# Linear attention into a gated feed-forward layer on one core: MoE chunks that end at token tiles, and the remainders of both quads as one unit

## The chip, the cores and the metric

The kernel runs on one core of a Trainium2 chip. The time is that of one execution on the device, in microseconds; lower is better. A core has TensorE (PE: matmuls; its loading of stationary operands is shown apart as PEld), VectorE (DVE), ScalarE (ACT), GpSimd (POOL), SyncE (SP: issues the DMAs here), an on-chip memory SBUF of 128 partitions, and 8 accumulator banks (PSUM) that TensorE writes and VectorE and ScalarE read.

## What is computed

```python
# 8 batches, 8 heads, 576 tokens, head dimension 64, 128 features; all float32
def phi(x):
    proj = np.einsum('bhsd,df->bhsf', x, w_phi)
    proj = proj - np.max(np.abs(proj), axis=-1, keepdims=True)
    return np.concatenate([np.exp(proj), np.exp(-proj)], axis=-1)
q_p, k_p = phi(q), phi(k)
kv = np.einsum('bhsf,bhsd->bhfd', k_p, v)
z = np.sum(k_p, axis=2)
num = np.einsum('bhsf,bhfd->bhsd', q_p, kv)
den = np.einsum('bhsf,bhf->bhs', q_p, z)[..., None] + 1e-06
x = (num / den).transpose(0, 2, 1, 3).reshape(B, S, 512)     # 8 x 576 tokens, 512 wide
h = np.maximum(x @ w_in, 0.0)                                 # 512 -> 1024
conv_out = sum(conv_w[k] * shift(h, k - 1) for k in range(3)) # over tokens, zeros at a batch's ends
gate = 1.0 / (1.0 + np.exp(-conv_out))
out = h * gate @ w_out                                        # 1024 -> 512
```

(The sum over shifts is the reference's loop over the three taps, written short.)

## The kernel before

**Attention.** The 8 heads of a batch form two *quads* (qd 0 and 1) of four heads; a quad is two pairs of two heads each, laid side by side in the partitions (64 + 64). A head's 576 tokens are four tiles of 128 and a remainder of 64. A *unit* is one batch, one quad, and one of three token groups: h = 1 and h = 2 hold two full tiles of both pairs, h = 0 the remainders of both pairs. `k_unit` loads keys and values, projects (`project`: pk), takes the largest absolute value (mk, L433, VectorE), subtracts it (sk, L440, VectorE), makes both exponentials (ke, L464, ScalarE; batch 0 by a bias instead, L468), and accumulates features times values (kv, L477 and L484, TensorE). After h = 2 the sums go to SBUF (kvf, L491). `q_unit` projects likewise (pq, mq, sq), transposes on TensorE (tp, L509), makes the exponentials (qe, L513), multiplies by kvf (nm, L524), and divides on VectorE (dn, rc, x).

TensorE works in three tilings: the whole array (128 x 128: transpositions, MoE, and the remainder's projection L413, one matmul of 256 columns for a quad), halves (128 x 64: kv, nm) and quarters (64 x 64: the projections of full tiles, L422, four at a time). A float32 matmul shows in the profile as two records.

**MoE.** The tokens of two batches are cut into three *chunks* of 384; there are 12. `x_part` transposes a chunk's token tiles on TensorE (xt, L564; a tile of which only a column or a few are needed goes as a matmul by part of the identity, L566) and splits the result into a rounded part and the rest (xh on ScalarE, xl on VectorE), 386 columns, since the convolution looks one token to each side. `h_part` has 8 groups f of 12 matmuls (hp, L594: 4 slices p of the width, three products each of the split weights and x), the relu (h, L598, ScalarE), the middle tap on GpSimd (c, L599), the two others on VectorE (L606), one sigmoid for the chunk (L611, ScalarE; it needs a change of the function table, 12 of them), the gate (L614, VectorE), and the split into gh (ScalarE) and gl (VectorE). `o_part` has 4 x 24 matmuls (op, L644), an eviction (os, L649) and the store. The weights come as 64-bit numbers and are rounded in the first part of the run on VectorE, ScalarE and GpSimd (w_t, win_lo, wout_lo).

**Order.** Every operation is put on a list with its engine, an expected cost, its reads and writes, and a rank. `Plan.order` then plays the list: at each step it takes the engine that can start earliest, and there, among what could start at that moment, the lowest rank; on TensorE `mode` stays in a tiling while something is ready for it. What comes out is the order on each engine, fixed in the program. Buffers have a number of slots, and an operation whose tile finds none free is put later: hidden tiles h have NHH slots, kv uses two PSUM banks, hp and op share two (M), and the other four (G) serve the rest.

Of the kernel before, what the change touches and what calls it, by code (L numbers as in the profile page):

```python
# [245 lines left out]
def kernel(  # L246
# [143 lines left out]
    QUAD = 470  # L390

    def project(src, b, qd, h, kind, r):
# [3 lines left out]
        if h == 0:  # L396
            raw = [piece([P, P], F32, f"r{nm}", "raw", RAW)]
            dma(lambda: raw[0](), lambda: src[b, qd, :, 512 : 512 + P], 64, r - 3.0, writes=w_(raw[0]))
            ps = [psum([P, 2 * F], f"p{nm}", G)]
            n = 2  # L400
        else:
            raw = [piece([P, 2 * P], F32, f"r{nm}_{pr}", "raw", RAW) for pr in range(2)]
            for pr in range(2):
# [4 lines left out]
            n = 4
        m = [piece([P, 2, n], F32, f"m{nm}_{i}", "m", 6) for i in range(len(ps))]
        pr_ = [None if biased else piece([P, n, F], F32, f"s{nm}_{i}", kind + "s", KS if kind == "k" else QS)  # L410
               for i in range(len(ps))]
        if h == 0:
            mm(432, lambda: nc.tensor.matmul(out=ps[0](), lhsT=raw[0](), rhs=wbd_f(), start=True, stop=True),  # L413
               w_(raw[0], wbd_f), w_(ps[0]), r, takes=(m[0],) if biased else (m[0], pr_[0]))
# [336 lines left out]
```

## Time and profile before

| | |
|---|---|
| time, median of 3 runs | 734.47 us (734.21 to 734.63) |
| the profiled execution: its time, its span | 734.25 us, 732.5 us |
| TensorE busy | 715.0 us, 98% of the span |
| VectorE busy | 491.1 us, 67% |
| ScalarE busy | 392.3 us, 54% |
| GpSimd busy | 104.7 us, 14% |
| granted TensorE clock | full, all the time |
| moved by DMA | 49.02 MB |

The span reaches from the first to the last instruction; the time adds 1.75 us around it. A group's row gives line, engine, operation, what is written from what, shapes and count, then busy time in us and mean duration in ns of one, then the idle time of the engine just before them and what ended it. Matmuls overlap in the array, so a mean duration is longer than the step from one start to the next.

### The profile page before, as it was taken

The numbers are of one execution on the slowest core, as the hardware profiler recorded it, in microseconds if no ns is written. First come the engines' busy times: TensorE is split into PE (matmuls) and PEld (weight loads), VectorE is DVE, ScalarE is ACT, GpSimd is POOL, SyncE is SP. The second block draws the span as 40 slices with busy tenths as digits, with TensorE's granted clock in tenths as the row PEclk, the third lists the DMA queues.
The fourth block names the chain that finished last, engine by engine and source line by source line (L and its number), as shares of the span: only waits on it lengthen the run. The fifth ranks groups of instructions, "written<-read, shape, count | busy, mean of one in ns | idle before, by whom it ended". The sixth has DMA issues, their size and how long they took to land.

```text
span 732.5 us, 22234 instructions
## 1 busy us (share of the span) xinstructions
PE 715.0 (98%) x9548; PEld 674.1 (92%) x9548; DVE 491.1 (67%) x1066; ACT 392.3 (54%) x740; POOL 104.7 (14%) x135
## 2 busy tenths in 40 slices
PE   8878999999999999999999999999999999999997
PEld 6767988899999999999999999999999999999997
DVE  3699899999685546657656687568574655576450
ACT  6976676874646426536435554554563544436251
POOL 1233334242001020010010002010001101020100
PEclk9999999999999999999999999999999999999999
DMA  8454444221230201103221231023121010000011
GB/s 239 129 173 135 140 138 129 64 72 37 82 100 18 60 12 60 49 11 93 71 59 33 79 88 42 33 79 85 46 66 34 19 34 17 27 2 34 12 33 44
DMA packets 46610, 49.02 MB, mean 67 GB/s; under 512 B 5296, under 2 KB 44464, under 8 KB 46512
## 3 DMA queue, kind: packets, MB, share of 16 engines
q1 hardware_dynamic: 46512, 47.59, 22.2%
q8 instruction: 76, 1.25, 0.7%
q14 instruction: 22, 0.18, 0.1%
HBM read 38.13 MB, written 9.44 MB: 65 GB/s over the span
## 4 chain that ended last, share of the span: by engine, by line
PE 89%; ACT 5%; DVE 4%; DMA 0%; issue 0%; POOL 0%; SPq 0%; ACTq 0%
PE op L644 28%; PE hp L594 27%; PE nm L524 9%; PE kv L484 6%; PE tp L509 4%; PE pq L422 4%; PE pk L422 3%; PE xt L564 3%; ACT ke L468 3%; PE kv L477 2%; PE pk L413 1%; PE pq L413 1%; DVE mk L433 1%; DVE mq L433 0%; DMA rk<-in_kT_dram 0%; DVE w_t L329 0%
## 5 line engine op out<-in xcount | busy, mean ns | idle before, releaser
L606 DVE SCALAR_TENSOR_TENSOR c<-h,cw,c 128x384 f32<-128x384 f32 (+3 forms) x256 | 128.9, 530 | 82.8 <-POOL c L599 81.0
L594 PE MATMUL hp<-xh,win_hi 128*128 128x386 f32 x384 | 136.1, 355 | 0.0
L644 PE MATMUL op<-gh,wout_hi 128*128 128x384 f32 x384 | 133.4, 347 | 0.0
L599 POOL TENSOR_SCALAR c<-h,cw 128x384 f32<-128x384 f32 x96 | 61.8, 646 | 498.0 <-ACT h L598 449.4
L594 PE MATMUL hp<-xl,win_hi 128*128 128x386 f32 x384 | 130.1, 339 | 1.1 <-DVE xl L572 1.1
L644 PE MATMUL op<-gl,wout_hi 128*128 128x384 f32 x384 | 130.2, 339 | 0.0
L594 PE MATMUL hp<-xh,win_lo 128*128 128x386 f32 x384 | 129.9, 338 | 0.0
L644 PE MATMUL op<-gh,wout_lo 128*128 128x384 f32 x384 | 129.6, 337 | 0.0
L598 ACT ACTIVATE h<-hp 128x386 f32<-128x386 f32 x96 | 47.2, 494 | 127.2 <-PE hp L594 127.1
L464 ACT ACTIVATE ke<-sk 128x512 f32<-128x512 f32 (+1 forms) x140 | 74.8, 594 | 51.2 <-DVE sk L440 28.8
L513 ACT ACTIVATE qe<-tp 128x512 f32<-128x512 f32 (+1 forms) x160 | 79.6, 570 | 35.0 <-PE tp L509 34.7
L524 PEld LDWEIGHTS nm<-kvf,qe 128*64 128x64 f32 x2304 | 71.9, 138 | 12.3 <-issue 9.4
L524 PE MATMUL nm<-kvf,qe 128*64 128x65 f32 x2304 | 79.2, 224 | 3.2 <-DVE sk L440 1.8
L594 PEld LDWEIGHTS hp<-xh,win_hi 128*128 128x128 f32 x384 | 72.3, 188 | 2.1 <-issue 1.2
L594 PEld LDWEIGHTS hp<-xl,win_hi 128*128 128x128 f32 x384 | 72.3, 188 | 1.5 <-DVE xl L572 1.5
L644 PEld LDWEIGHTS op<-gh,wout_hi 128*128 128x128 f32 x384 | 72.2, 188 | 1.5 <-issue 1.0
L594 PEld LDWEIGHTS hp<-xh,win_lo 128*128 128x128 f32 x384 | 72.5, 189 | 0.3
L644 PEld LDWEIGHTS op<-gl,wout_hi 128*128 128x128 f32 x384 | 72.1, 188 | 0.2 <-DVE gl L626 0.2
L644 PEld LDWEIGHTS op<-gh,wout_lo 128*128 128x128 f32 x384 | 72.2, 188 | 0.1
L484 PE MATMUL kv<-v,ke 128*64 128x65 f32 x2048 | 71.3, 223 | 0.3 <-ACT ke L468 0.2
L484 PEld LDWEIGHTS kv<-v,ke 128*64 128x64 f32 x2048 | 65.4, 138 | 4.4 <-ACT ke L468 1.7
L433 DVE TENSOR_REDUCE mq<-pq 128x4 f32<-128x512 f32 (+1 forms) x80 | 48.6, 630 | 30.1 <-PE pq L422 20.8
(62 smaller groups left out, 960.9 us busy)
## 6 DMA issues: line engine op xcount, KB each, us to landing
v<-in_vt_dram SPq DMA_DIRECT2D x80, 130.0 KB, 2.3
rk<-in_kT_dram SPq DMA_DIRECT2D x64, 128.0 KB, 2.5
rq<-in_qT_dram SPq DMA_DIRECT2D x64, 128.0 KB, 2.3
out_dram<-os SPq DMA_DIRECT2D x32, 192.0 KB, 1.9
w_r<-in_w_in_dram SPq DMA_DIRECT2D x8, 512.0 KB, 3.9
w_r<-in_w_out_dram SPq DMA_DIRECT2D x8, 512.0 KB, 3.9
out_dram<-os SPq DMA_DIRECT2D x32, 96.0 KB, 1.7
rk<-in_kT_dram SPq DMA_DIRECT2D x16, 64.0 KB, 2.5
```

What stands on the lines that cost most here:

```text
L422: nc.tensor.matmul(out=ps[i]()[a : a + 64, (2 * pr + t) * F : (2 * pr + t + 1) * F], lhsT=raw[pr]()[rows, t * P + a : t * P + a + 64], rhs ...
L433: lambda i=i, view=view: nc.vector.tensor_reduce(out=m[i]()[:, 0], in_=view(), axis=AX, op=ALU.max, apply_absolute_value=True), w_(p), [(m ...
L464: act(*((630, 522) if n == 4 else (416, 307)), lambda s=s, e=e, j=j: nc.scalar.activation(out=e[s](), in_=pr[j](), func=AF.Exp, scale=1.0 ...
L484: nc.tensor.matmul(out=kp[j]()[a : a + 64, s, t // 2 * VW : (t // 2 + 1) * VW], lhsT=e[s]()[:, t, a : a + 64], rhs=vs[t // 2]()[:, c : c + ...
L509: nc.tensor.transpose(out=tp()[:, t, :], in_=pr[j]()[:, t, :], identity=idn())
L513: act(*((597, 478) if n == 4 else (384, 264)), lambda s=s, tp=tp, qe=qe: nc.scalar.activation(out=qe()[:, s], in_=tp(), func=AF.Exp, scale ...
L524: nc.tensor.matmul(out=ps_()[a : a + 64, t, :], lhsT=qe()[:, s, t, a : a + 64], rhs=kv[b, qd][t if h == 0 else j]()[:, s, p0 : p0 + VW], s ...
L594: nc.tensor.matmul(out=ps(), lhsT=w, rhs=x, start=(p == 0 and k == 0), stop=(p == 3 and k == 2))
L598: act(494, 373, lambda ps=ps, hs=hs: nc.scalar.activation(out=hs(), in_=ps(), func=AF.Relu), w_(ps), w_(hs), rf)
L599: pool(590, 557, lambda f=f, hs=hs: nc.gpsimd.tensor_scalar(out=c4()[:, f, :], in0=hs()[:, o : o + TC], scalar1=cwv()[:, f, 1:2], scalar2= ...
L606: lambda f=f, hs=hs, j=j, lo=lo, hi=hi: nc.vector.scalar_tensor_tensor(out=c4()[:, f, lo:hi], in0=hs()[:, o + j - 1 + lo : o + j - 1 + hi] ...
L644: nc.tensor.matmul(out=ps(), lhsT=w, rhs=x, start=(i == 0), stop=(i == 23))
```

## The change

Chunks now follow the token stream of all batches (4608 tokens) and end where a token tile ends: 11 chunks, of 384, 448 or 320 tokens. A chunk's hidden layer is computed for its own columns alone. The convolution's output lags two tokens behind the chunk's end (but not at a batch's end), and the three hidden columns that the next chunk needs from this one are copied by GpSimd into the front of its hidden tile. The remainders of both quads of a batch form one unit (k or q), projected in quarters like the full tiles. xh and xl are tiles of their own for each p. Numbers of slots change (hidden tiles 10 to 9, x 8 to 6, raw 6 to 5, v 4 to 2 and two for the remainder, qe 2 to 3), and so do the planner's costs and ranks (of which a few lines stand here).

```diff
-TC = 384
-HW = TC + 2
-HSTART = (0, 383, 766)
-NCH = 12
+EDGE = [64 * n for n in (0, 6, 13, 20, 27, 33, 40, 47, 54, 60, 67, 72)]
+NCH = len(EDGE) - 1
+HW = 448
+TC = HW + 2
-QORDER = [(0, 1), (1, 1), (0, 2), (1, 2), (0, 0), (1, 0)]
+QORDER = [(0, 1), (1, 1), (0, 2), (1, 2), (0, 0)]
+KORDER = [(0, 0), (0, 1), (0, 2), (1, 1), (1, 2)]
-LEAD = 36.0
+LEAD = 42.0
-NHH = 10
+NHH = 9
 def project(src, b, qd, h, kind, r):
-        if h == 0:
-            raw = [piece([P, P], F32, f"r{nm}", "raw", RAW)]
-            dma(lambda: raw[0](), lambda: src[b, qd, :, 512 : 512 + P], 64, r - 3.0, writes=w_(raw[0]))
-            ps = [psum([P, 2 * F], f"p{nm}", G)]
...
-            mm(432, lambda: nc.tensor.matmul(out=ps[0](), lhsT=raw[0](), rhs=wbd_f(), start=True, stop=True),
-               w_(raw[0], wbd_f), w_(ps[0]), r, takes=(m[0],) if biased else (m[0], pr_[0]))
+        n, w = (1, P) if h == 0 else (2, 2 * P)
+        for u in range(2):
+            q, c0 = (u, 512) if h == 0 else (qd, u * 640 + (h - 1) * 256)
+            dma(lambda u=u: raw[u](), lambda q=q, c0=c0: src[b, q, :, c0 : c0 + w], w // 2, r - 3.0, writes=w_(raw[u]))
...
+        def emit(u):
+            for t in range(n):
+                for a in (0, 64):
+                    for i in range(2):
+                        rows = slice(i * D, i * D + D)
+                        nc.tensor.matmul(out=ps[i]()[a : a + 64, (n * u + t) * F : (n * u + t + 1) * F],
+                                         lhsT=raw[u]()[rows, t * P + a : t * P + a + 64],
+                                         rhs=wbd_f()[rows, i * F : i * F + F], start=True, stop=True)
+def around(n):
+        w0, w1 = EDGE[n], EDGE[n + 1]
+        a, z = w0 - 2 * (w0 % S > 0), w1 - 2 * (w1 % S > 0)
...
 def x_part(n, r):
+        tiles = [(b, t, b * S + t * P - w0) for b in range(B) for t in range(5) if w0 <= b * S + t * P < w1]
...
-                    if first + col - i >= 0 and first + col - i + P <= 512:
-                        nc.tensor.transpose(out=xt()[:, first + col - i : first + col - i + P], in_=x, identity=idn())
-                    else:
-                        nc.tensor.matmul(out=xt()[:, first + col : first + col + w], lhsT=x, rhs=idn()[:, i : i + w],
-                                         start=True, stop=True)
+                    nc.tensor.transpose(out=xt()[:, at : at + P], in_=q()[:, qd if t == 4 else 2 * pr + t % 2],
+                                        identity=idn())
 def h_part(n, r):
-                        nc.tensor.matmul(out=ps(), lhsT=w, rhs=x, start=(p == 0 and k == 0), stop=(p == 3 and k == 2))
+                        nc.tensor.matmul(out=ps()[:, :W], lhsT=w, rhs=x, start=(p == 0 and k == 0),
+                                         stop=(p == 3 and k == 2))
+            if t0 < w0:
+                old = hold[f]
+                pool(130, 100, lambda hs=hs, old=old: nc.gpsimd.tensor_copy(
+                    out=hs()[:, :3], in_=old[0]()[:, w0 - old[1] : w0 - old[1] + 3]), [(old[0], "h")], [(hs, "carry")], rf)
```

In k's remainder unit the products with the values (L477 before, L466 now) are issued for one quad after the other, 8 matmuls each as before. The order on the engines changes throughout; three places follow. In the names the first number after the letters is the batch (or the chunk, for xt, hp, h, c and op), then quad and group.

TensorE, the key remainders of batch 5 before: one for each quad, each one matmul of the whole array, the second 157 rows behind the first.

```order
L422 MATMUL pq4_0_1_1_5243<-wbd_f_66,rq4_0_1_1_4646 64x128
L413 MATMUL pk5_0_0_5262<-wbd_f_66,rk5_0_0_4688 128x256
L644 MATMUL op3_3_5230<-gh3_0_4702,wout_hi2_2021 128x384
...
L509 MATMUL tp4_0_2_1_5747<-idn_111,sq4_0_2_1_5711 128x128 x4
L413 MATMUL pk5_1_0_5756<-wbd_f_66,rk5_1_0_5446 128x256
L594 MATMUL hp5_0_5759<-xh5_5602,win_hi0_236 128x386
```

The same remainders now:

```order
L597 MATMUL hp3_2_4760<-xl3_0_4450,win_hi0_374 128x448
L409 MATMUL pk5_0_0_0_4767<-wbd_f_66,rk5_0_0_0_4653 64x128
L409 MATMUL pk5_0_0_1_4769<-wbd_f_66,rk5_0_0_0_4653 64x128
L409 MATMUL pk5_0_0_0_4767<-wbd_f_66,rk5_0_0_0_4653 64x128
L409 MATMUL pk5_0_0_1_4769<-wbd_f_66,rk5_0_0_0_4653 64x128
L409 MATMUL pk5_0_0_0_4767<-wbd_f_66,rk5_0_0_1_4687 64x128
L409 MATMUL pk5_0_0_1_4769<-wbd_f_66,rk5_0_0_1_4687 64x128
L409 MATMUL pk5_0_0_0_4767<-wbd_f_66,rk5_0_0_1_4687 64x128
L409 MATMUL pk5_0_0_1_4769<-wbd_f_66,rk5_0_0_1_4687 64x128
L480 MATMUL kv4_1_0_4234<-v4_1_2_0_4626,ke4_1_2_0_1_4723 64x65 x4
```

Two whole-array matmuls became eight in quarters, between whole-array and half-array work.

TensorE, the second chunk's transpositions (chunk 1, its first slice p) and its last hidden group with the first output matmul behind it, before:

```order
L564 MATMUL xt1_0_2133<-idn_111,x0_0_0_1413 128x128
L566 MATMUL xt1_0_2133<-idn_111,x0_0_2_1070 128x1
L564 MATMUL xt1_0_2133<-idn_111,x0_0_2_1070 128x128
L564 MATMUL xt1_0_2133<-idn_111,x1_0_1_1736 128x128 x2
...
L594 MATMUL hp1_7_3108<-xl1_2187,win_hi3_787 128x386
L644 MATMUL op0_0_3133<-gh0_0_2729,wout_hi0_1561 128x384
```

and now:

```order
L568 MATMUL xt1_0_2573<-idn_91,x0_0_0_1352 128x128
L568 MATMUL xt1_0_2573<-idn_91,x0_0_2_1008 128x128
L568 MATMUL xt1_0_2573<-idn_91,x1_0_1_1632 128x128 x2
...
L597 MATMUL hp1_7_3583<-xl1_3_2810,win_hi3_913 128x448
L654 MATMUL op0_0_3605<-gh0_0_3148,wout_hi0_1630 128x382
```

The single column is gone, and the matmuls are wider. Ahead of that first output matmul stand, now, pq3_1_1 and pk4_0_1; before, pk3_1_1 came only behind it.

GpSimd, the end of the first chunk's middle tap and the start of the second's, before:

```order
L599 TENSOR_SCALAR c0_1557<-h0_7_2470,cw_240 128x384
L343 TENSOR_TENSOR w13_t_2351<-w13_t_2351 128x512
L386 TENSOR_TENSOR wout_lo5_2525<-w13_t_2351,wout_hi5_2512 128x512
L343 TENSOR_TENSOR w14_t_2523<-w14_t_2523 128x512
L386 TENSOR_TENSOR wout_lo6_2789<-w14_t_2523,wout_hi6_2766 128x512
L343 TENSOR_TENSOR w15_t_2533<-w15_t_2533 128x512
L386 TENSOR_TENSOR wout_lo7_2947<-w15_t_2533,wout_hi7_2924 128x512
L599 TENSOR_SCALAR c1_3014<-h1_0_2569,cw_240 128x384
```

and now:

```order
L609 TENSOR_SCALAR c0_1628<-h0_7_2591,cw_235 128x382
L343 TENSOR_TENSOR w12_t_2485<-w12_t_2485 128x512
L604 COPY h1_1_2749<-h0_1_1608 128x3
...
L604 COPY h1_7_2798<-h0_7_2591 128x3
L386 TENSOR_TENSOR wout_lo4_2801<-w12_t_2485,wout_hi4_2795 128x512
L604 COPY h2_0_2883<-h1_0_2467 128x3
L343 TENSOR_TENSOR w13_t_2733<-w13_t_2733 128x512
L386 TENSOR_TENSOR wout_lo5_3003<-w13_t_2733,wout_hi5_2979 128x512
```

The copies of the carried columns stand in the queue ahead of the rounding of the last output weights.

More of the change, by code (lines that the diff above doesn't have):

```diff
@@ L409, in project @@
[L409 to L413, printed above, removed]
-               w_(raw[0], wbd_f), w_(ps[0]), r, takes=(m[0],) if biased else (m[0], pr_[0]))
-        else:
-            def emit(pr):
-                for t in range(2):
-                    for a in (0, 64):
-                        for i in range(2):
-                            rows = slice(i * D, i * D + D)
-                            nc.tensor.matmul(out=ps[i]()[a : a + 64, (2 * pr + t) * F : (2 * pr + t + 1) * F],
-                                             lhsT=raw[pr]()[rows, t * P + a : t * P + a + 64],
-                                             rhs=wbd_f()[rows, i * F : i * F + F], start=True, stop=True)
-            for pr in range(2):
-                mm(QUAD, lambda pr=pr: emit(pr), w_(raw[pr], wbd_f), [(ps[0], pr), (ps[1], pr)], r + 0.01 * pr,
-                   takes=[x for x in (*m, *pr_) if x is not None], tiled=2)
@@ L429, in project @@
+        for u in range(2):
+            mm(225 * n, lambda u=u: emit(u), w_(raw[u], wbd_f), [(ps[0], u), (ps[1], u)], r + 0.01 * u,
+               takes=[x for x in (*m, *pr) if x is not None], tiled=2)
         for i, p in enumerate(ps):
[L430 removed]
+            ri = r + n * i
             view = lambda p=p: p().rearrange("p (t f) -> p t f", f=F)
[L432 removed]
+            vec(*((681, 597) if n == 2 else (417, 331)),
                 lambda i=i, view=view: nc.vector.tensor_reduce(out=m[i]()[:, 0], in_=view(), axis=AX, op=ALU.max,
@@ new lines, in around, with cols @@
+    def around(n):
+        w0, w1 = EDGE[n], EDGE[n + 1]
+        a, z = w0 - 2 * (w0 % S > 0), w1 - 2 * (w1 % S > 0)
+        spans = []
+        for k in (0, 1):
+            cut = sorted({a, z, *(t for b in range(B + 1) for t in (b * S - k, b * S - k + 1) if a <= t <= z)})
+            spans.append([(lo, hi) for lo, hi in zip(cut, cut[1:]) if not (hi == lo + 1 and (lo + k) % S == 0)])
+        return w0, w1, a, z, spans
+    def cols(fixed, each, n, more):
+        return fixed + each * n + more, fixed + each * n
@@ L569, in x_part @@
-            mm(115 * len(tiles), emit, w_(idn, *dict.fromkeys(xs[q] for q in src)), w_(xt), r, takes=(xh[n], xl[n]))
-            act(494, 373, lambda p=p, first=first, xt=xt: nc.scalar.activation(
-                out=xh[n]()[:, p], in_=xt()[:, first : first + HW], func=AF.Copy), w_(xt), [(xh[n], p)], r)
-            vec(550, 466, lambda p=p, first=first, xt=xt: nc.vector.tensor_tensor(
-                out=xl[n]()[:, p], in0=xt()[:, first : first + HW], in1=xh[n]()[:, p].bitcast(F32),
-                op=ALU.subtract), [(xt, None), (xh[n], p)], [(xl[n], p)], r)
@@ L576, with emit @@
-    gt = {}
+            src = [xs[b, qd, 0 if t == 4 else 1 + t // 2] for b, t, _ in tiles]
+            def emit(qd=qd, pr=pr, src=src, first=first, xt=xt):
+                for (b, t, c), q in zip(tiles, src):
+                    at = first + c - (pr * 64 if t == 4 else 0)
+                    nc.tensor.transpose(out=xt()[:, at : at + P], in_=q()[:, qd if t == 4 else 2 * pr + t % 2],
+                                        identity=idn())
+            mm(109 * len(tiles), emit, w_(idn, *dict.fromkeys(src)), w_(xt), r, takes=(xh[n, p], xl[n, p]))
```

239 lines of the change are left out of this document (118 added, 121 removed).

## The prediction

> **What bounds the kernel now.** I read the page first: share of each engine, the slices, the chain that ended last. TensorE is busy for 715.0 of 732.5 us and carries 89% of the chain; its slices stand at 9 from the fifth to the last but one, at full clock. VectorE is the only other engine near its limit, and only in slices 3 to 10 (each is 18.3 us).
>
> ```profile
> PE 715.0 (98%) x9548; PEld 674.1 (92%) x9548; DVE 491.1 (67%) x1066; ACT 392.3 (54%) x740; POOL 104.7 (14%) x135
> PE   8878999999999999999999999999999999999997
> DVE  3699899999685546657656687568574655576450
> PEclk9999999999999999999999999999999999999999
> PE 89%; ACT 5%; DVE 4%; DMA 0%; issue 0%; POOL 0%; SPq 0%; ACTq 0%
> ```
>
> Then the busy times by stage. The columns are the stretch, its length, and busy time with instruction count of PE, PEld, DVE, ACT, POOL.
>
> ```profile
> 0.00:70.00 70.00, 58.66 (x1219) 49.01 (x1219) 50.45 (x107) 54.07 (x150) 18.69 (x21) 1.00 0.60 174
> 70.00:180.00 110.00, 107.62 (x1834) 98.51 (x1834) 104.59 (x231) 73.72 (x141) 37.75 (x34) 1.00 0.34 98
> 180.00:728.00 548.00, 548.00 (x6496) 526.17 (x6495) 336.10 (x730) 264.02 (x449) 48.22 (x80) 1.00 0.16 47
> 728.00:732.50 4.50, 0.73 (x5) 0.40 (x3) 0.00 (x0) 0.49 (x1) 0.00 (x0) 1.00 0.12 44
> ```
>
> From 180 to 728 us TensorE never idles: a microsecond of its work removed there is a microsecond of time. From 70 to 180 it idles for 2.4 us, beside a VectorE that is busy for 104.6 of 110. Before 70 us it idles for 11.3 us and waits for others, so work removed there buys nothing unless the waits go too. The last 4 us are the final eviction and its store. Of all that TensorE waits for, the list of waits has a result of VectorE at the top (time in all, times, longest):
>
> ```profile
> PE tp L509 <- DVE sq L440: 1.9, 2, 1.4
> ```
>
> **The change part by part.** Because matmuls overlap, I price them by the step from one start to the next, not by their durations. First the remainder units. Groups by line, and the same two groups in the first 70 us alone, count the records (two records are one float32 matmul here: 16 units, 32 records of each kind):
>
> ```profile
> L413 PE MATMUL pk<-wbd_f,rk 128*128 128x256 f32 x32 | 10.7, 418 | 2.5 <-DMA rk<-in_kT_dram 1.4 <-DVE mk L433 1.0
> L413 PE MATMUL pq<-wbd_f,rq 128*128 128x256 f32 x32 | 9.6, 386 | 0.5 <-PE hp L594 0.5
> ...
> L413 PE MATMUL pk<-wbd_f,rk 128*128 128x256 f32 x8 | 3.3, 494 | 2.5 <-DMA rk<-in_kT_dram 1.4 <-DVE mk L433 1.0
> L413 PE MATMUL pq<-wbd_f,rq 128*128 128x256 f32 x4 | 1.3, 398 | 0.0
> ```
>
> Timeline rows (start, length, line, what, count) give the steps:
>
> ```profile
> 250.73 0.59 PE L413 MATMUL pk<-wbd_f,rk 128*128 128x256 f32 x2
> 251.16 1.47 PE L564 MATMUL xt<-idn,x 128*128 128x128 f32 x12
> 252.39 0.42 PE L644 MATMUL op<-gh,wout_hi 128*128 128x384 f32 x1
> 252.65 0.34 PE L644 MATMUL op<-gh,wout_lo 128*128 128x384 f32 x1
> ...
> 439.17 0.34 PE L594 MATMUL hp<-xh,win_hi 128*128 128x386 f32 x1
> 439.35 0.33 PE L594 MATMUL hp<-xh,win_lo 128*128 128x386 f32 x1
> 439.52 0.34 PE L594 MATMUL hp<-xl,win_hi 128*128 128x386 f32 x1
> 439.79 1.10 PE L422 MATMUL pq<-wbd_f,rq 64*64 64x128 f32 x32
> 440.71 1.05 PE L422 MATMUL pk<-wbd_f,rk 64*64 64x128 f32 x32
> 441.70 1.11 PE L477 MATMUL kv<-v,ke 128*64 128x130 f32 x16
> 442.74 0.45 PE L594 MATMUL hp<-xh,win_hi 128*128 128x386 f32 x1
> 443.03 0.34 PE L594 MATMUL hp<-xh,win_lo 128*128 128x386 f32 x1
> ```
>
> A whole-array remainder projection holds TensorE from 250.73 to 251.16, 0.43 us; two of them, one for each quad, 0.86. The merged unit has 8 quarter matmuls, 16 records. A run of 32 such records that is followed by more of them takes 439.79 to 440.71, 0.92 us, so 16 take 0.46. The saving is 0.40 us for each of 16 merged units: **-6.4 us**. Their reductions, subtractions and exponentials keep their number and width, and so do the remainder matmuls with the values and the transpositions of q; the stores and loads are a few more on a queue whose engines are busy for at most a third after 70 us, and I cost them at nothing.
>
> Second, the transpositions of x. Chunks of 386 columns cut token tiles: a chunk needs 4, 5 and 4 tiles in turn (13 for two batches), and in the second kind one is a matmul of a single column. Where chunks end at tile ends there are 40 tiles, 160 transpositions instead of 192 and no single columns.
>
> ```profile
> L564 PE MATMUL xt<-idn,x 128*128 128x128 f32 x192 | 27.9, 276 | 1.0 <-ACT qe L513 0.9
> L566 PE MATMUL xt<-idn,x 128*128 128x1 f32 x32 | 4.5, 209 | 0.0
> ...
> 300.49 0.63 PE L564 MATMUL xt<-idn,x 128*128 128x128 f32 x4
> 300.96 0.28 PE L566 MATMUL xt<-idn,x 128*128 128x1 f32 x2
> 301.10 0.63 PE L564 MATMUL xt<-idn,x 128*128 128x128 f32 x4
> ```
>
> Twelve transpositions hold from 251.16 to 252.39, and the first matmul behind them steps by 0.26 instead of 0.18: 1.31 us, 0.109 each. A set of five, the single column in it, steps from 300.49 to 301.10, 0.61. Before: 16 x 0.61 + 32 x 4 x 0.109 = 23.7 us. After: 160 x 0.109 = 17.4. Saved: **-6.3 us**.
>
> Third, the MoE matmuls: 96 of each kind in every chunk, 12 chunks before and 11 after, 192 fewer, while the columns stay 4608 for the output and fall from 4632 to 4608 for the hidden layer. At 0.175 us for 386 columns (439.17 to 439.52, halved) pure proportion gives 24 x 96 x 0.175 / 386 = 1.0 us, the small end. A fixed part in each matmul would add 192 times itself. The nearest rows that show one are the float32 records: 256 columns step by 0.215 (half of 0.43), 128 by 0.109, which leaves 0.003 us and a total of 1.6. The large end takes 128 columns at 0.109 and 386 at 0.175 as one line: 0.076 us fixed, a total of 15. They are different kinds of matmul, so I stay by the near row and round up: **-2.0 us**. The Trainium skill, "TensorE: Matmul & The Clock Gate", section "Wait — 56ns, not 53.3ns?", has warm matmuls step by columns over 2.4 GHz plus about 2.5 ns; that would be 163 ns for 386 columns, and the trace's 175 disagrees. If all that stands above 161 ns is fixed, an estimate from that page, this term would be 3.7 us.
>
> Fourth, the order. Counting TensorE's changes among whole array, halves (kv, nm) and quarters in the two orders, I find 182 before and 197 after, since a remainder now enters the quarters. The rows price one: hp to quarters 0.27 for 0.18, quarters to kv 0.99 for 0.92, kv to hp 0.29 for 0.18; so 0.07 to 0.11. I take 0.10 x 15 = **+1.5 us** (1.0 to 1.7 by these rows; twice that if the neighbours' records hide as much again). The Trainium skill, "TensorEngine Tiling (Array Packing)", section "Key Properties", says that changing the tiling mode drains TensorE. That speaks against the remainder in quarters, and the rows agree that each change costs, though far less than the 0.40 us gained; with about 0.17 us, the warm latency on the TensorE page's "Single matmul latency", as an estimate, the term would be 2.5.
>
> Sum on TensorE: -6.4 - 6.3 - 2.0 + 1.5 = -13.2 us. What falls before 70 us I don't count: six whole-array projections (the 8 + 4 records), 3 x 0.40 = 1.2, and the first chunk's 12 instead of 16 transpositions, 0.4. So **+1.6** back, and -11.6 in all.
>
> GpSimd gets 64 copies of three columns. It is busy for 104.7 of 732.5 us, which covers them. Each waits for a free hidden tile, of which there are 9 instead of 10, and what is behind it in the queue waits too; at the second chunk that is the rounding of the last output weights:
>
> ```profile
> L343 POOL TENSOR_TENSOR w_t<-w_t 128x512 f32<-128x512 f32 x16 | 21.0, 1315 | 78.0 <-DVE w_t L339 63.8 <-DVE rc L532 7.9 <-DVE dn L530 6.3
> L386 POOL TENSOR_TENSOR wout_lo<-w_t,wout_hi 128x512 fp32r<-128x512 f32 x8 | 11.0, 1381 | 8.1 <-ACT wout_hi L385 8.1
> ```
>
> Behind the copies stand 4 of the second and 3 of the first kind, 9.5 us, and the first output matmul needs them. Between the same tiles' release and that matmul TensorE has 7 groups of 12 hidden matmuls, 84 x 0.2 = 17 us, which hide it. What the tiles themselves cost is the last rival's ground. ScalarE's table changes go from 12 sigmoids to 11, off the path.
>
> **The rivals.**
>
> *The VectorE stage eats more.* From 70 to 180 us it is busy for 95%. The new order runs attention further ahead: pq3_1_1 and pk4_0_1 stand before the first output matmul, where before pk3_1_1, half a batch less, was still to come. Attention leans on VectorE, so the dense stage lasts longer. For it speaks the row 70 to 180; against it that TensorE idled for only 2.4 of 110 us there. Price: the savings inside it (by the order 3 pairs of remainders 1.2, the second chunk's transpositions 0.7, MoE 0.4: 2.3 us) and another 2.4 us of waits, up to 3.7: -11.6 + 2.3 + 2.4 to 3.7, 727.5 to 729 by the median.
>
> *The early waits go as well.* The first 70 us hold 11.3 us of TensorE idle, and their order is new too. If half of it went, with the 1.6 us kept: -11.6 - 1.6 - 5.7, about 715.5. Nothing in the rows says that it does: VectorE's load there (50.45 us) is unchanged.
>
> *The carried columns stall the hidden layer: slower.* With 9 tiles the second hidden matmul group of a chunk waits until the gate of the chunk before has released a tile.
>
> ```profile
> L598 ACT ACTIVATE h<-hp 128x386 f32<-128x386 f32 x96 | 47.2, 494 | 127.2 <-PE hp L594 127.1
> L599 POOL TENSOR_SCALAR c<-h,cw 128x384 f32<-128x384 f32 x96 | 61.8, 646 | 498.0 <-ACT h L598 449.4 <-DVE sk L440 46.6 <-DVE dn L530 2.0
> L606 DVE SCALAR_TENSOR_TENSOR c<-h,cw,c 128x384 f32<-128x384 f32 x64 | 39.7, 620 | 35.7 <-POOL c L599 34.9
> L611 ACT ACTIVATE c<-c 128x3072 f32<-128x3072 f32 x12 | 33.3, 2773 | 2.3 <-DVE c L606 2.2
> L611 ACT ACT_TABLE_LOAD x12 | 15.4, 1283 | 12.0 <-DVE c L606 11.8
> L614 DVE TENSOR_TENSOR c<-c,h 128x384 f32<-128x384 f32 x96 | 47.6, 551 | 28.9 <-ACT c L611 28.9
> ```
>
> The chain from the last hidden matmul: 0.49 + 0.65 + 2 x 0.62 + 1.28 + 2.77 x 448/384 + 0.55 x 448/384 = 7.5 us. Its cover at a chunk's end is mostly one chunk's output, 72 matmuls or more at 0.175 and longer, 12.6 us; only at the first boundary there are attention units instead. It decides once ten boundaries lose 1.2 us each; at 1.6 each the time is 739. The cover speaks against it.
>
> **How the numbers follow.** The profiled execution took 734.25 us (span 732.5); -11.6 makes 722.65, and since the median of the runs lies 0.2 above it, 722.8. Likeliest, TensorE's sum with the early part lost: 0.61, from 719.5 (a fixed part of some 15 ns in each MoE matmul, fewer early losses) to 726 (the early part lost twice, changes of tiling at twice their price). The early waits go too: 0.14. VectorE's stage: 0.18. Within 0.2% of before (1.5 us, about what a measurement of this kernel can tell from no change): 0.02. The carried columns: 0.05. The range 716 to 729 leaves out somewhat over half of the early-waits case, a quarter of VectorE's, and the last two. Faster 0.93, same 0.02, slower 0.05.
>
> **What the profile after would show.** 1152 quarter records in the remainder's place and 0.46 us for a unit; 160 transpositions and no single columns; MoE steps of 0.203 us for 448 columns if nothing in them is fixed, and less if something is; TensorE full from about 190 us to the end; its idle time before 70 us about 11 to 13 us and up to 180 us no more than 3 more. The prediction is wrong if idle time between 70 and 180 us grows beyond 5 us, if TensorE waits for GpSimd's copies or for ScalarE's hidden tiles at chunk ends, or if 448 columns step by more than 0.205 us.

## The result, and the profile after

The changed kernel takes 718.26 us (median of 4 runs, 717.65 to 718.68); the kernel before took 734.55 us beside it (734.21 to 735.41). The ratio is 0.9776, with a 95% interval of 0.9759 to 0.9793: 16.3 us less, where 11.7 had been predicted (722.8, range 716 to 729). The profiled execution took 718.68 us, with a span of 716.9.

From the page of the profile after: the engines' shares, then the slices (17.9 us each now).

```profile
PE 700.0 (98%) x9484; PEld 636.8 (89%) x9484; DVE 488.8 (68%) x1050; ACT 384.1 (54%) x717; POOL 127.3 (18%) x191
PE   7998999999999999999999999999999999999998
DVE  3699999988969557755773576777457654765540
```

The busy times by stage, cut where they were cut before, with the same columns:

```profile
0.00:70.00 70.00, 60.24 (x1312) 51.23 (x1312) 51.34 (x118) 55.81 (x156) 20.20 (x22) 0.98 0.61 174
70.00:180.00 110.00, 107.54 (x2159) 95.89 (x2159) 101.68 (x221) 76.72 (x151) 33.85 (x40) 0.98 0.39 112
180.00:713.00 533.00, 531.79 (x6017) 489.44 (x6014) 335.74 (x713) 251.14 (x410) 73.24 (x129) 1.00 0.15 46
713.00:717.00 4.00, 0.48 (x4) 0.21 (x2) 0.00 (x0) 0.44 (x1) 0.00 (x0) 0.84 0.11 41
```

TensorE idles for 9.8, 2.5 and 1.2 us in the first three stretches (11.3, 2.4 and 0 before). In all it hardly waited less; it had less to do: 700.0 us busy instead of 715.0. The stretch from 70 to 180 us is as full as before, although it holds 2159 matmul records instead of 1834: work moved forward into it. The 0.98 in the first two stretches are two spells at half the full clock, from 9.2 to 12.6 and from 138.9 to 142.3 us (granted 0.50 in both); the kernel before has 1.00 from 0 to 728 us.

The groups that the change names. The remainders have become part of the 1152 quarter records of each kind, the transpositions are 160, the copies are there.

```profile
L409 PE MATMUL pk<-wbd_f,rk 64*64 64x128 f32 x1152 | 43.2, 284 | 2.2 <-DMA rk<-in_kT_dram 2.2
L409 PE MATMUL pq<-wbd_f,rq 64*64 64x128 f32 x1152 | 43.1, 280 | 2.9 <-DVE rc L530 1.6 <-DVE sk L427 1.3
L604 POOL COPY h<-h 128x3 f32<-128x3 f32 x64 | 25.9, 405 | 60.8 <-DVE c L623 51.5 <-DVE sk L427 5.2 <-POOL h L604 0.4
L568 PE MATMUL xt<-idn,x 128*128 128x128 f32 x160 | 21.9, 274 | 1.9 <-DVE sq L427 1.1 <-ACT qe L511 0.7
```

Rows of the timeline of TensorE show a merged remainder unit between hidden matmuls of 448 columns:

```profile
266.82 0.36 PE L597 MATMUL hp<-xh,win_lo 128*128 128x448 f32 x1
267.03 0.37 PE L597 MATMUL hp<-xl,win_hi 128*128 128x448 f32 x1
267.32 0.67 PE L409 MATMUL pq<-wbd_f,rq 64*64 64x128 f32 x16
267.92 0.48 PE L597 MATMUL hp<-xh,win_hi 128*128 128x448 f32 x1
268.24 0.37 PE L597 MATMUL hp<-xh,win_lo 128*128 128x448 f32 x1
268.44 0.37 PE L597 MATMUL hp<-xl,win_hi 128*128 128x448 f32 x1
```

A hidden matmul of 448 columns steps by 0.205 (268.24 to 268.44) where nothing else stands between. The unit holds the array from 267.32 to 267.92, 0.60 us; and its neighbours step by 0.29 and 0.32 instead of 0.205.

To see where the 15.6 us of the span went, I sorted the whole time of TensorE: each step from one start to the next goes to the kind of the matmul that began it; what a step near a change of tiling lasts beyond the usual step of its kind goes to the changes (after 25 us); what no matmul covers goes to idle. In us:

| | before | after | difference |
|---|---|---|---|
| projections, remainders among them | 67.0 | 63.7 | -3.3 |
| transpositions (of x and of q) | 52.3 | 46.1 | -6.2 |
| hidden layer | 207.2 | 201.6 | -5.6 |
| output | 205.2 | 204.1 | -1.1 |
| kv and nm | 138.5 | 136.4 | -2.1 |
| around changes of tiling | 34.1 | 38.8 | +4.7 |
| longer steps in the first 25 us | 7.9 | 6.5 | -1.4 |
| idle | 12.7 | 12.4 | -0.3 |
| head, tail and first matmuls | 7.7 | 7.3 | -0.4 |
| span | 732.6 | 716.9 | -15.7 |

The second slow spell falls on projections, where it lengthens the steps of 62 records by some 1.5 us in all; so the row of the projections is that much too high for the work alone.

### The profile page after: what moved, and what is told of

Same layout as the page of the kernel before. It is cut to its first block, busy times and chain, and to the rows that moved or that the text cites. A ratio compares the mean times of both kernels' runs of the same rounds, so it can differ in the third digit from the quotient of the medians.

```text
span 716.9 us, 22154 instructions
## 1 busy us (share of the span) xinstructions
PE 700.0 (98%) x9484; PEld 636.8 (89%) x9484; DVE 488.8 (68%) x1050; ACT 384.1 (54%) x717; POOL 127.3 (18%) x191
## 3 DMA queue, kind: packets, MB, share of 16 engines
q1 hardware_dynamic: 46512, 47.59, 22.5%
## 5 line engine op out<-in xcount | busy, mean ns | idle before, releaser
L615 DVE SCALAR_TENSOR_TENSOR c<-h,cw,c 128x381 f32<-128x381 f32 (+11 forms) x256 | 127.0, 533 | 71.6 <-POOL c L609 70.3
L609 POOL TENSOR_SCALAR c<-h,cw 128x448 f32<-128x448 f32 (+3 forms) x88 | 59.7, 680 | 402.1 <-ACT h L607 399.7
L597 PE MATMUL hp<-xh,win_hi 128*128 128x448 f32 (+2 forms) x352 | 130.2, 370 | 0.0
L654 PE MATMUL op<-gh,wout_hi 128*128 128x448 f32 (+3 forms) x352 | 127.7, 363 | 0.0
L654 PE MATMUL op<-gl,wout_hi 128*128 128x448 f32 (+3 forms) x352 | 124.4, 353 | 0.1
L654 PE MATMUL op<-gh,wout_lo 128*128 128x448 f32 (+3 forms) x352 | 124.3, 353 | 0.0
L597 PE MATMUL hp<-xh,win_lo 128*128 128x448 f32 (+2 forms) x352 | 123.7, 351 | 0.0
L597 PE MATMUL hp<-xl,win_hi 128*128 128x448 f32 (+2 forms) x352 | 123.6, 351 | 0.0
L607 ACT ACTIVATE h<-hp 128x448 f32<-128x448 f32 (+2 forms) x88 | 45.9, 523 | 123.1 <-PE hp L597 122.7
L635 DVE TENSOR_TENSOR gl<-c,gh 128x896 fp32r<-128x896 f32 (+3 forms) x44 | 43.5, 1026 | 38.3 <-ACT gh L632 38.3
```

The lines of the kernel that those rows point to most:

```text
L597: nc.tensor.matmul(out=ps()[:, :W], lhsT=w, rhs=x, start=(p == 0 and k == 0), stop=(p == 3 and k == 2))
L607: act(*cols(49, 0.84, W, 121), lambda ps=ps, hs=hs: nc.scalar.activation(out=hs()[:, 3 : 3 + W], in_=ps()[:, :W], func=AF.Relu), w_(ps), [ ...
L609: pool(*cols(240, 0.85, N, 30), lambda f=f, hs=hs: nc.gpsimd.tensor_scalar(out=c4()[:, f, :N], in0=hs()[:, at(t0) : at(t1)], scalar1=cwv() ...
L615: lambda f=f, hs=hs, j=j, lo=lo, hi=hi: nc.vector.scalar_tensor_tensor(out=c4()[:, f, lo - t0 : hi - t0], in0=hs()[:, at(lo) + j - 1 : at( ...
L635: vec(*cols(67, 1.04, 2 * N, 87), lambda f=f, a=a, gh4=gh4, gl4=gl4: nc.vector.tensor_tensor(out=gl4()[:, a : a + 2, :N], in0=c4()[:, f : ...
L654: nc.tensor.matmul(out=ps()[:, :N], lhsT=w, rhs=x, start=(i == 0), stop=(i == 23))
```

## The experiments

**The changed kernel once more**, on the chip of the next three.

> The changed kernel itself, run beside the next three on the same chip as their reference: 718.3 us, with the same orders on every engine.

Measured: 719.13 us (717.84 to 719.48), ratio 0.9779 (0.9765 to 0.9794), span 717.1. By the same sorting it idles for 13.7 us and its projections take 62.2 (its two slow spells lie before 23 us, in the row of the first 25), so single rows of that table are good to about 1.5 us. The runs below are compared with this one, and sums by the sorting too. They ran on three chips, on which the kernel before took 734.9, 735.4 and 734.6 us; differences across chips are uncertain by as much.

**The remainder in the whole array, planned so.** The merged unit stays, but it is projected by matmuls of the whole array, and the planner knows it.

```diff
+            if h == 0:
+                for i in range(2):
+                    nc.tensor.matmul(out=ps[i]()[:, u * F : (u + 1) * F], lhsT=raw[u](), rhs=wbd_f()[:, i * F : i * F + F], ...)
+                return
-            mm(225 * n, ... tiled=2)
+            mm(432 if h == 0 else 225 * n, ... tiled=0 if h == 0 else 2)
```

> The merged remainder unit stays, but its projection takes the whole array again (two matmuls of 128 columns for a quad, tiling 0 for the planner). The quarters were worth 16 x 0.40 = 6.4 us, and the order has 178 changes of tiling instead of 197. Theory A (TensorE's sum, a change of tiling costs 0.20 to 0.25 us as the boundaries in the trace after sum up): 6.4 less 19 x 0.20 to 0.25 = 3.8 to 4.8, so 1.6 to 2.6 us slower than the changed kernel, near 720.5. Theory B (the prediction's 0.10 us for a change): 6.4 - 1.9 = 4.5 us slower, near 722.8. Theory C (the gain is the new order's and its waits): no slower, 718.3 or less.

Measured: 734.58 us, ratio 0.9997 (0.9985 to 1.0009). The whole gain is gone, which the price of a projection cannot explain. TensorE idles for 20.7 us instead of 13.7, and one wait makes that difference. From the list of waits:

```profile
PE nm L527 <- DVE xl L579: 8.4, 1, 8.4
```

And the timeline of ScalarE, VectorE and TensorE at that place:

```profile
128.81 1.28 ACT L625 ACT_TABLE_LOAD   x1
130.10 2.75 ACT L625 ACTIVATE c<-c 128x3056 f32<-128x3056 f32 x1
...
132.89 4.90 DVE L628 TENSOR_TENSOR c<-c,h 128x382 f32<-128x382 f32 x8 [4.82 <-ACT c L625]
137.71 2.20 DVE L579 TENSOR_TENSOR xl<-xt,xh 128x448 fp32r<-128x448 f32 x4
...
128.82 1.11 PE L471 MATMUL kv<-v,ke 128*64 128x130 f32 x16
138.37 1.90 PE L527 MATMUL nm<-kvf,qe 128*64 128x65 f32 x30 [8.45 <-DVE xl L579]
```

It is the first chunk boundary. The gate of chunk 0 goes through ScalarE (table, sigmoid, 4 us) and VectorE (8 products, 4.9 us); the rests xl stand in VectorE's row behind the products; and in this order TensorE has nothing ahead of the nm that waits for them. From 134.7 to 141.5 us, during the wait and behind it, the granted clock is 0.50, which lengthens the loss. So this run tells nothing on quarters against whole array. It shows a stall at the place, and by the gate's chain, that the prediction's third rival names; but what TensorE waits for is VectorE's row, not a free hidden tile or a copied column.

**Twelve chunks that end at token tiles.**

```diff
-EDGE = [64 * n for n in (0, 6, 13, 20, 27, 33, 40, 47, 54, 60, 67, 72)]
+EDGE = [64 * n for n in (0, 6, 13, 18, 24, 31, 36, 42, 49, 54, 60, 67, 72)]
```

> Twelve chunks instead of eleven, all still ending at token tiles (320, 384 and 448 tokens in turn): 192 more MoE matmuls over the same columns, the transpositions unchanged at 160. Theory A (a fixed 13.5 ns in every MoE matmul, as the steps 147, 173 and 200 ns for 320, 384 and 448 columns say): 192 x 0.0135 = 2.6 us slower than the changed kernel, 720.9. Theory B (the prediction's near row, 3 ns fixed): 0.6 us slower, 718.9. Theory C (smaller chunks let the order wait less): faster than 718.3.

Measured: 721.58 us (721.22 to 723.54), ratio 0.9821 (0.9805 to 0.9837): 2.45 us more than the changed kernel for 192 more MoE matmuls and the same number of columns, 12.8 ns each. The steps of hidden matmuls in the changed kernel are 146.7, 173.5 and 201.6 ns for 320, 384 and 448 columns: the first two make 0.42 ns a column and 12.7 fixed, the last two 0.44 and 5. The time agrees with theory A. But the 384 hidden matmuls of 448 columns step by 203.1 ns in this run, which is 0.6 of the 2.45 us; without that the fixed part is some 10 ns, as a mean of hidden and output matmuls.

**Another pitch of gh and gl.** Their rows lie 464 columns apart instead of 450.

```diff
-gh4 = piece([P, 4, TC], F32R, f"gh{n}_{f}", "gh", 2)
+gh4 = piece([P, 4, 464], F32R, f"gh{n}_{f}", "gh", 2)
```

(gl4 in the same way.)

> The rows of gh and gl lie 464 numbers apart instead of 450 (a multiple of 64 bytes, as xh's and xl's 448 are), TensorE's order the same row for row. In the trace after, hidden matmuls of 448 columns step by a near constant 200 ns and output matmuls of 448 by 197 to 209, mean 203.6. Theory A (the start of a row matters): output steps fall to about 200.6, 1056 x 2.5 to 3 ns = 2.6 to 3.2 us faster, 715.3. Theory B (it is something else, as the clean 64-byte rows of gh before did not make the 384-column steps even): no change, 718.3.

Measured: 720.92 us, ratio 0.9808 (0.9794 to 0.9822). The output matmuls of 448 columns step by 203.9 ns as before (203.6): the pitch is not what makes them longer than hidden ones. The run is 1.8 us slower than the changed kernel, which neither theory has; hidden matmuls of 448 columns step by 203.1 instead of 201.6 ns, 1.0 us for 672 of them.

**The remainder in the whole array, order kept.** The edit of the second run, without telling the planner: TensorE's order stays, with the whole-array matmuls in the quarters' place.

> The remainder's projection takes the whole array again, but the planner is told that it is in quarters at its old cost, so that every engine's order stays that of the changed kernel row for row. Changes of tiling on TensorE fall from 197 to 176. Theory A (work and changes of tiling alone, each change 0.20 to 0.25 us): + 6.4 - 21 x 0.20 to 0.25 = 1.2 to 2.2 us slower than the changed kernel, 719.9 to 721.3. Theory B (each change 0.10, as predicted): + 6.4 - 2.1 = 4.3 us slower, 723.4. Theory C (the projection in quarters is itself worth the 15 us that the first whole-array run lost): 734. If it is A or B, that run's loss was its order's.

Measured: 720.42 us (720.09 to 721.72), ratio 0.98 (0.9787 to 0.9813), span 718.8: 1.3 us slower by the medians, 1.7 by the spans. Here the same unit stands between the same neighbours:

```profile
267.67 0.37 PE L602 MATMUL hp<-xl,win_hi 128*128 128x448 f32 x1
267.88 1.05 PE L407 MATMUL pq<-wbd_f,rq 128*128 128x128 f32 x8
268.69 0.45 PE L602 MATMUL hp<-xh,win_hi 128*128 128x448 f32 x1
268.98 0.37 PE L602 MATMUL hp<-xh,win_lo 128*128 128x448 f32 x1
```

From the hidden matmul ahead of the unit to the second one behind it, 267.67 to 268.98 is 1.31 us; in quarters it was 267.03 to 268.24, 1.21. So this merged unit gains 0.10 us in quarters. The array's own time is 0.81 against 0.46, but the two changes of tiling take 0.25 of the 0.35 back.

That holds where whole-array matmuls stand on both sides. Where half-array work follows, the whole-array unit has a change of tiling of its own behind it. One such unit in the changed kernel, then here:

```profile
275.56 0.36 PE L597 MATMUL hp<-xl,win_hi 128*128 128x448 f32 x1
275.85 0.67 PE L409 MATMUL pk<-wbd_f,rk 64*64 64x128 f32 x16
276.45 1.15 PE L480 MATMUL kv<-v,ke 128*64 128x65 f32 x32
...
276.28 0.36 PE L602 MATMUL hp<-xl,win_hi 128*128 128x448 f32 x1
276.48 1.05 PE L407 MATMUL pk<-wbd_f,rk 128*128 128x128 f32 x8
277.46 1.15 PE L485 MATMUL kv<-v,ke 128*64 128x65 f32 x32
```

From the hidden matmul to kv it is 0.89 us in quarters and 1.18 in the whole array: 0.29 gained. After 100 us there are six units of each kind; the six gain 0.09 to 0.11 us each, the other six 0.29 to 0.30, 2.4 us in all. The run lost less than that, and it idled for 12.1 us, 1.5 less than the changed kernel in its second profile.

**Thirty-two more changes of tiling**: in each remainder unit one matmul of a single column of the whole array, in the middle of the quarters.

```diff
+            if h == 0 and u == 1:
+                nc.tensor.matmul(out=ps[0]()[:, F : F + 1], lhsT=raw[1](), rhs=wbd_f()[:, 0:1], start=True, stop=True)
```

> In the middle of each of the 16 merged remainder projections stands a whole-array matmul of one column whose result is overwritten: 32 changes of tiling more (229), the rest of the order unchanged. The one-column matmul itself takes 0.17 us, as 0.61 - 4 x 0.109 in the trace before: 2.8 us for 16. Theory A (0.20 to 0.25 us for a change): 6.4 to 8 us + 2.8 = 9.2 to 10.8 us slower than the changed kernel, 728.3 to 729.9. Theory B (0.10): 3.2 + 2.8 = 6.0, 725.1.

Measured: 725.47 us (724.14 to 727.03), ratio 0.9866 (0.985 to 0.9882): 6.3 us more by the medians, 0.20 for a change with its share of the small matmul; by the two profiled spans 8.2. At each of the twelve units after 100 us the time that the unit holds the array grows by 0.47 us (from 0.60 to 1.07), 7.6 if all sixteen pay it; less the 0.17 of the small matmul it is 0.15 for a change, not 0.07 to 0.11.

**The chunks alone** (the old remainder units, the new planner's numbers) and **the units alone** (the old chunks, the old numbers).

> The 11 chunks, with the remainders left as they were, one unit for each quad, one whole-array matmul each; the planner's numbers are the changed kernel's. 180 changes of tiling. Theory A (TensorE's sum): transpositions -6.3, MoE matmuls -4.2 (13.5 ns fixed, and 24 columns), changes of tiling 0: 10.5 us faster than before, 724.2. Theory B (the prediction's size for MoE): 8.3 faster, 726.4. Theory C (the gain beyond the sum lies in the planner's new numbers): another 2 to 3 us below A.

> The merged remainder units in quarters, with the old 12 chunks and the old planner's numbers (two value buffers instead of four, with two for the remainder, to fit). 200 changes of tiling. Theory A: -6.4 + 18 x 0.20 to 0.25 = 1.9 to 2.8 us faster than before, 732 to 733. Theory B (0.10 for a change): 4.6 faster, 730.2. Theory C (merging helps the early waits): below 730.

Measured: 741.24 us, ratio 1.0076 (1.0055 to 1.0096), and 742.42 us, ratio 1.0092 (1.0078 to 1.0107). Each half of the change alone is slower than the kernel before. The windows (same columns) of the chunks alone and of the units alone:

```profile
0.00:70.00 70.00, 54.17 (x1101) 46.58 (x1103) 44.86 (x92) 50.37 (x142) 16.81 (x19) 0.90 0.52 154
70.00:180.00 110.00, 103.34 (x1491) 92.57 (x1487) 97.06 (x201) 66.59 (x125) 43.80 (x45) 0.98 0.33 93
```

```profile
0.00:70.00 70.00, 57.88 (x1272) 50.18 (x1272) 50.00 (x110) 54.43 (x151) 20.61 (x22) 0.98 0.62 175
70.00:180.00 110.00, 100.77 (x1822) 89.95 (x1822) 96.37 (x204) 68.73 (x132) 34.47 (x33) 0.94 0.34 97
```

TensorE idles for 22.5 and 21.3 us before 180 us (12.2 in the changed kernel), in different places, and its granted clock falls there to 0.90 and 0.94. In each, 17 us before 180 us lie in spells at half the full clock (6.8 in the changed kernel). From 180 to 740 us they idle for 5 and 3 us, most of the tail included. So both lost time before 180 us, in waits and slow clock. That the order is the cause is not shown by these two runs: 6.7 us of the waits of the chunks alone are for loads of values, which have fewer slots in my edit than before. The last four runs ask what another order does.

**The changed kernel with the planner's numbers of before.** The same work in another order.

```diff
-SWITCH = {(0, 1): 100, (0, 2): 130, (1, 0): 100, (2, 0): 10, (1, 2): 100, (2, 1): 150}
+SWITCH = {(0, 1): 250, (0, 2): 250, (1, 0): 120, (2, 0): 120, (1, 2): 200, (2, 1): 200}
-LEAD = 42.0
-WIN0 = 5.0
-WIN = 4.0
+LEAD = 36.0
+WIN0 = 0.0
+WIN = 5.0
-HQ = 2
+HQ = 1
```

> The changed kernel with all planner's numbers of before (LEAD 36, WIN0 0, WIN 5, HQ 1, the old costs of a change of tiling): the same work in another order; TensorE changes its tiling 196 times (197 in the changed kernel), so that this does not differ. Theory A, the order is half of the gain (the two parts alone lost 7 and 8 us by their orders): TensorE idles for 4 to 10 us more, most of it before 180 us, and the time is 722 to 729. Rival B, the numbers matter little and the removed work carries the gain wherever it stands: idle within 2 us of the changed kernel's 12.4, time 717 to 721.

Measured: 728.5 us (726.99 to 729.82), ratio 0.9917 (0.9901 to 0.9932). Theory A holds: with the same work, the numbers alone make 9 to 10 us. The largest wait is again at the first chunk boundary. From the list of waits, and from the summary of VectorE's products there (count, then the shortest, median and longest in ns):

```profile
PE tp L507 <- DVE sq L427: 6.6, 2, 6.2
```

```profile
L623 DVE TENSOR_TENSOR c<-c,h x8: 543/546/1625, 132.2 to 138.0; 128x382 f32<-128x382 f32 x8
```

The timeline of VectorE, GpSimd and TensorE:

```profile
132.22 6.36 DVE L623 TENSOR_TENSOR c<-c,h 128x382 f32<-128x382 f32 x8 [0.56 <-ACT c L620]
138.51 1.27 DVE L420 TENSOR_REDUCE mq<-pq 128x4 f32<-128x512 f32 x2
139.71 1.27 DVE L427 TENSOR_TENSOR sq<-pq,mq 128x512 f32<-128x512 f32 x2
...
134.11 1.59 POOL L386 TENSOR_TENSOR wout_lo<-w_t,wout_hi 128x512 fp32r<-128x512 f32 x1
135.65 0.51 POOL L604 COPY h<-h 128x3 f32<-128x3 f32 x1
136.12 1.58 POOL L386 TENSOR_TENSOR wout_lo<-w_t,wout_hi 128x512 fp32r<-128x512 f32 x1
...
140.53 1.94 PE L507 MATMUL tp<-idn,sq 128*128 128x128 f32 x8 [6.21 <-DVE sq L427]
```

TensorE's next work, a transposition of q, needs a subtraction that stands in VectorE's row behind the gate's eight products. In the changed kernel the same gate passes at 134 us, the hidden matmuls of chunk 1 and an nm stand beside it, and TensorE waits for 1.6 us:

```profile
134.26 3.81 DVE L623 TENSOR_TENSOR c<-c,h 128x382 f32<-128x382 f32 x8
...
134.87 3.25 POOL L604 COPY h<-h 128x3 f32<-128x3 f32 x7 [1.15 <-DVE c L623]
...
134.92 0.37 PE L597 MATMUL hp<-xh,win_lo 128*128 128x448 f32 x1
135.13 0.36 PE L597 MATMUL hp<-xl,win_hi 128*128 128x448 f32 x1
135.42 1.46 PE L522 MATMUL nm<-kvf,qe 128*64 128x65 f32 x32
136.81 0.43 PE L409 MATMUL pq<-wbd_f,rq 64*64 64x128 f32 x2
138.82 1.75 PE L409 MATMUL pq<-wbd_f,rq 64*64 64x128 f32 x27 [1.59 <-DVE rc L530]
```

Idle in all is 4 us more (17.7 against 13.7), no more than this wait adds, and the spans differ by 8.3; the rest lies in longer steps (hidden matmuls 1.5, changes 1.8, the first 25 us 1.0 by the sorting). Part of these is the clock: it is 0.50 from 139.2 to 146.0 us, at the wait's end and behind it, twice as long as in the changed kernel.

**The chunks alone and the units alone, with planner's numbers chosen for each.**

```diff
 # the chunks alone
-LEAD = 42.0
+LEAD = 40.0
-M0 = 10.0
+M0 = 12.0
...
 # the units alone
-LEAD = 36.0
+LEAD = 34.0
-NT = 4
+NT = 5
...
```

(In both: the costs of a change of tiling 140 to 205, STAY 200, and smaller changes of the other ranks.)

> The new chunks with the old remainder units (as in the run of the chunks alone, 741.24 us), and planner's numbers chosen for it; 174 changes of tiling instead of 180. Theory A, the chunks remove 10 us (transpositions 5.9, MoE 4.2) and the earlier run lost them to an order full of waits: idle back to 12 to 15 us, granted clock back over 0.99, time 722 to 727. Rival B, the chunks' own buffers (9 hidden tiles, carried columns) make the waits whatever the order: idle over 18 us, time 733 or more.

> The merged remainder units with the old chunks (as in the run of the units alone, 742.42 us), and planner's numbers chosen for it; 177 changes of tiling instead of 200. Theory A, the units are worth little by themselves (1.3 to 1.8 us by the run with the order kept) and 23 changes fewer give 3 to 5: idle 12 to 15 us, time 728 to 733. Rival B, two value tiles and the merged unit's longer lists of inputs make the waits whatever the order: idle over 18 us, time 736 or more. Rival C, the prediction's 6.4 us in full, with no more waits: 725 to 728.

Measured: the chunks alone 732.57 us (730.64 to 734.5), ratio 0.9971 (0.996 to 0.9982); the units alone 729.92 us (728.75 to 731.43), ratio 0.9935 (0.9921 to 0.995). Another order gave back 8.7 and 12.5 us, and the units come out at theory A's time (with 15.8 us idle, a little over its 12 to 15). The chunks do not: at 732.57 they miss theory A (722 to 727) and stay just short of B's time (733 or more), with the idle time that B expects, 21.6 us. The two largest waits of TensorE make half of it:

```profile
PE kv L484 <- DMA v<-in_vt_dram: 6.5, 5, 2.8
PE tp L509 <- DVE sq L440: 4.2, 6, 1.6
```

In the changed kernel values have two slots and the remainders' values two of their own; in my two kernels of the chunks alone the old units put both into two slots (before there were four), and TensorE waits for their loads. Those 6.5 us belong to my edit. Hidden matmuls step by 204.9 ns for 448 columns there, 3.3 more than in the changed kernel, which is another 3 us. What the chunks alone are worth without both was not run.

**Other planner's numbers for the changed kernel**, which leave 177 changes of tiling instead of 197.

```diff
-LEAD = 42.0
-WIN0 = 5.0
-WIN = 4.0
+LEAD = 38.0
+WIN0 = 8.0
+WIN = 5.0
...
```

> The changed kernel with other planner's numbers (LEAD 38, WIN0 8, WIN 5, HQ 3, and costs of a change of tiling nearer to the measured ones, 140 to 205): the same work, 177 changes of tiling instead of 197. Theory A, a change costs 0.20 us and the order waits as little as before: 20 x 0.20 = 4 us less, 714 to 716. Rival B, 0.11 for each: 2.2 us less, 716 to 717.5. Rival C, as with the two parts alone a new order brings waits that eat it: idle 3 us or more above 12.4, time 718 or more.

Measured: 718.9 us (717.39 to 720.18), ratio 0.9783 (0.9767 to 0.9799), no better than the changed kernel (0.9776 and 0.9779). Rival C has the time but not the reason: idle is 12.5 us. By the sorting 3.7 to 3.9 us were saved around the changes of tiling, as theory A has it, and other steps grew longer. Most of what ate the gain is the clock. The profiled execution has four spells of 3.4 us at half the full clock, from 19.2, 43.1, 67.0 and 193.3 us; the changed kernel has two. In the last of them output matmuls of 382 columns step by 316 to 320 ns instead of 175, so a spell of 3.4 us filled with work costs about 1.5 us, and two more cost some 3. The first 70 us and the last spell:

```profile
0.00:70.00 70.00, 59.25 (x1233) 51.62 (x1234) 47.46 (x104) 52.47 (x147) 16.55 (x19) 0.93 0.56 163
193.30:196.70 3.40, 3.40 (x13) 3.39 (x12) 3.16 (x8) 3.12 (x1) 0.00 (x0) 0.50 0.26 77
```

The fastest of the four executions, 717.39 us, has a mean granted clock of 0.998, the three others 0.990. What sets a spell off in one order and not in another is not shown: the kernel before idles for 11.3 of its first 70 us without one.

No version that I ran beats the changed kernel.

## Why the prediction was right, and where only in sum

The bound was read rightly: TensorE was full after 180 us, so removed work was removed time, and VectorE's dense stage did not get longer. Of what was named as signs of an error none came: 2.5 us idle from 70 to 180 us, no wait of TensorE for the copies, 0.2016 us for 448 hidden columns. Two of its other marks missed: a unit holds the array for 0.60 us instead of 0.46, and the first 70 us idle for 9.8 instead of 11 to 13. But the 16 us come from terms that miss in both directions, and that the sum came out near is in part luck: the remainder and the changes of tiling were 6.3 us worse than forecast, everything else together 10.4 better (MoE 4.7, kv and nm 2.1, the early part 1.6, the first 25 us 1.4, the rest 0.6).

- **Transpositions, -6.3.** Measured -6.2. Right, and the whole of it is time.
- **Remainder in quarters, -6.4, and the changes of tiling, +1.5.** Together -4.9 was predicted; the sorting shows -3.3 and +4.7, a loss of 1.4 (about nothing without the slow spell on the projections). The +4.7 is the whole order's, not the remainders' alone. The pair with the order kept shows where it went: of some 0.31 us forecast for a unit, 0.10 is gained between whole-array matmuls, and 0.29 only where half-array work follows. The step that failed is the price of a change, 0.07 to 0.11: I read it at the entry into the quarters (0.27 for 0.18) and took the 0.46 from a run of records that is followed by more of the same tiling. A unit between hidden matmuls pays at three steps, 0.09 ahead, 0.14 within its last step (0.60 for 0.46) and 0.11 behind; behind a whole-array unit, too, 0.09 of that is paid (0.29 for 0.205). Over the twelve units after 100 us the quarters themselves give 2.4 us, where 3.7 had been forecast.
- **MoE, -2.0.** Measured -4.2 by steps and counts (hidden -3.7, output -0.5), -6.7 with the first steps of groups. The mis-sized term is the fixed part of a matmul: I took the near row, 3 ns, and the run with twelve chunks shows 10 to 13, near the 15 that I had kept for the range. The rows were float32 records, and their line does not carry over to these matmuls. But the fixed part is not all of the -4.2. For the output it is 5 to 10 ns by the widths (148.4, 175.1 and 203.6 ns for 322, 382 and 448 columns), which fits its -0.5. Hidden matmuls stepped by 176.4 ns for 386 columns before, 2 ns above the line of 320 and 384 columns after, and that alone is 2.3 us of their -3.7 (0.9 goes back, since 448 columns lie 1.3 ns above the line). It belongs to the steps without a known cause in the last section. The Trainium skill, "TensorE: Matmul & The Clock Gate", section "Wait — 56ns, not 53.3ns?", gives about 2.5 ns to a warm matmul; here the widths and the run with twelve chunks show 5 to 13 ns for these, and the measurement decides.
- **The early part, +1.6 back.** It was not lost: the first 70 us idle for 9.8 instead of 11.3 us, because work moved forward into them (1312 records instead of 1219). That is a quarter of what the second rival needed (5.7).
- **Not foreseen:** kv and nm 2.1 us shorter, and 1.4 us of shorter steps in the first 25 us; against them the spells at half clock, of which the second cost about 1.5 us and which the kernel before does not have.
- **The rivals.** VectorE's stage is as it was (101.7 of 110 us busy, TensorE waits for 2.5). The carried columns stalled nothing in the changed kernel. But the third rival's place and chain are real: at the first chunk boundary, where the prediction saw only attention units as cover, two other orders (one with the remainder in the whole array) lost 8.4 and 6.2 us behind the gate, in VectorE's row and not by the carried columns.

What the prediction did not price at all is the order. It read the order of the changed kernel and found no new wait in it; so the forecast held. But the planner's numbers, which stand in the diff as a few lines, decide over 9 to 10 of the 16 us: with those of before, the same work takes 728.5. They are not a gain of their own, for the changed kernel idles as long as the kernel before (12.4 and 12.7 us); they keep the new work from waiting. The kernel before was not run with other numbers, so what a new order alone would give the old work stays open. Why this order waits so little is shown only at that boundary; for the rest it stays open, and that the forecast met an order without new waits is luck as far as these runs tell.

## What to carry to other kernels

Price a change of tiling over the whole visit, from the last matmul of the old tiling to the second one behind it, and against the same visit without it; between hidden matmuls here the entry alone shows 0.09 of 0.34 us. Look, too, at what stands behind the visit: in front of another tiling the same visit gained three times as much. Where a planner sets the order, a part of a change cannot be tested by taking the other part out: judge it with the order kept, or with an order chosen anew for each. Compare the granted clock as well as the idle time, since two orders that idle alike can differ by slow spells. Look first at the first boundary of a stage, where an engine's row of gate work can stand ahead of what TensorE needs next.
